# Attention scores: one 128-key product per head on half of the array's rows, in place of two 64-key products on quarters

## The chip, the cores and the metric

The kernel runs on one core of one Trainium2 chip. The metric is the device time of one execution in microseconds (us), lower is better. The engines of the core are named as in the profile: PE (TensorE, matrix products), PEld (its weight loads), DVE (VectorE), ACT (ScalarE), POOL (GpSimd) and SP (which issues most of the DMAs).

## The reference

A linear attention with a decay per head feeds a mixture of experts in two levels (4 groups of 4 experts, one expert per token). B=4, H=8, S=768, D=64; 3072 tokens of 512 features, hidden width 1024.

```python
for t in range(S):
    state = gamma * state + einsum('bhd,bhe->bhde', k[:, :, t], v[:, :, t])
    y[:, :, t] = scale * einsum('bhd,bhde->bhe', q[:, :, t], state)
x = y.transpose(0, 2, 1, 3).reshape(B * S, H * D)
# per token: best group g, best expert e in it, with softmax weights g_w and e_w
out[tok] = g_w * e_w * (relu(x[tok] @ w1[g, e]) @ w2[g, e])
```

## The kernel before

**Stages.** The attention stage fills about the first 105 us. After it the kernel goes through the 16 experts one by one: tokens are gathered, transposed and sent through the two products of the expert's network, each split into a high and a low half of 16 bits. The instruction order of every engine is written out by hand (`manual_schedule`), so each engine works through its queue in the order in which the Python code issues it.

**The attention stage.** The sequence is cut in chunks of 128 tokens. There are 12 steps `i` (NS2): each takes one chunk of two of the four batch rows, `u` = 0 and 1. A step's queries, keys and values arrive by DMA (`load`, issued three or four steps ahead). The heads are held as four pairs `p`; the two heads of a pair, `par` = 0 and 1, lie on partitions 0 to 63 and 64 to 127, because a head has 64 features. All products of this stage are of 32-bit floats, and the trace shows two matmul records (two passes) for each of them, with a weight load for each; transposes have one.

The parts of a step, in the names of the code and with their lines in the profile:

- `score_mm(i, u)` (L240) makes the products of keys and queries within a chunk, for one `u`. Keys are the stationary operand (weights), queries the moving one. The result lies with keys on partitions and queries along the columns, in one PSUM bank `sh[2u + par]` for each `par`.
- `score_mask` (L252, DVE) multiplies a bank by the causal mask `tri` into `pf`; two instructions of 128x512 for each call of `score_mm`. Where a key is later than the query, `tri` is 0.
- `value_out` (L304) multiplies `pf` with the values, `state_out` (L291) multiplies the queries with the carried state, both into `op`; `state_mm` (L266) adds the chunk to the state.
- `keys_mm` (L225) and `trans_mm` (L350) are transposes, `logits_mm` (L324) and `select_mm` (L337) make the router's logits. `tally` (L555) and `route` (L444, L446) place the tokens.

**The quarters.** In a chunk the first 64 keys matter to all 128 queries, the last 64 keys only to the last 64 queries. `score_mm` uses this: for each head it issues a product of 64 keys with 128 queries and one of 64 keys with 64 queries, and leaves out the quarter of late keys and early queries. Each product takes 64 rows (features) and 64 columns (keys) of the array, so the four products of a pair take its four quarters. The order of the keys on the partitions is turned by 64 for every second pair (`KEYS`, and `tri[:, 1]` for the mask), so that the longer products go to either column half in turn. A call issues 4 pairs x 2 x 2 = 16 products, 32 passes.

**The order around it.** In step `i` from 2 to 10 the queue of PE is: `score_mm(i+1, 0)`, now and then `tally` or late `select_mm`, `state_out(i, ·)` (not where a sequence begins), `score_mm(i+1, 1)`, `value_out(i, 0)`, `value_out(i, 1)`, `state_mm`, `logits_mm(i-1)`, transposes, `select_mm`. Steps 0 and 1 issue the two calls of the next step back to back. There are 24 calls of `score_mm` in all. The mask of a call is used by `value_out` one step later.

Of the kernel before, what the change touches and what calls it, by code (L numbers as in the profile page):

```python
# [22 lines left out]
P = 128  # L23
# [88 lines left out]
class Kernel:  # L112
# [115 lines left out]
    def score_mm(self, i, u):  # L228


        nc, s = self.nc, self.st[i]
        qT, kT = s["q"][:, u], s["k"][:, u]
        for p in range(4):
            for late in range(2):
                for par in range(2):
                    half = (late + p) % 2
                    rs = slice(64 * par, 64 * par + 64)
                    ks = p * P + 64 * half
                    cs = slice(p * P + 64 * late, p * P + P)
                    nc.tensor.matmul(  # L240
                        self.sh[2 * u + par][64 * half:64 * half + 64, cs], kT[rs, ks:ks + 64], qT[rs, cs],
                        start=True, stop=True, skip_group_check=True,
                    )

    def score_mask(self, i, u):
        nc, s = self.nc, self.st[i]
# [1315 lines left out]
```

## Time and profile before

| | |
|---|---|
| median of 3 runs | 398.45 us (397.72 to 401.91) |
| the profiled execution, its own time | 397.01 us |
| its span in the trace | 395.3 us |
| what lies around the span | 1.7 us |
| PE busy | 383.5 us, 97% of the span |
| DVE, ACT, POOL busy | 289.1, 224.0, 159.5 us |
| mean granted clock of PE | 0.997 |

The span is the time from the first to the last instruction in the trace. Matrix products overlap one another, and their ends are modelled; a group's busy time is the union of its records, and the distance from the first start of one group to the first start of the next is what the group took from PE. That distance is used below. The chain of work that ended last follows the execution back from its last instruction, at each step to what released it.

### The profile page before, as it was taken

The numbers are of one execution on the slowest core, as the hardware profiler recorded it, in microseconds if no ns is written. First come the engines' busy times: TensorE is split into PE (matmuls) and PEld (weight loads), VectorE is DVE, ScalarE is ACT, GpSimd is POOL, SyncE is SP. The second block draws the span as 40 slices with busy tenths as digits, with TensorE's granted clock in tenths as the row PEclk, the third lists the DMA queues.
The fourth block names the chain that finished last, engine by engine and source line by source line (L and its number), as shares of the span: only waits on it lengthen the run. The fifth ranks groups of instructions, "written<-read, shape, count | busy, mean of one in ns | idle before, by whom it ended". The sixth has DMA issues, their size and how long they took to land.

```text
span 395.3 us, 14260 instructions
## 1 busy us (share of the span) xinstructions
PE 383.5 (97%) x5945; PEld 324.0 (82%) x5977; DVE 289.1 (73%) x480; ACT 224.0 (57%) x342; POOL 159.5 (40%) x172
## 2 busy tenths in 40 slices
PE   8999999999999999999999999999999999999992
PEld 4889889878869878888888879797887978869791
DVE  3675776858879969795868686776978769788620
ACT  2234534534744766666666566676776767667620
POOL 5542669567866216141516234241530413412112
PEclk9999999999999999999999999999999999999998
DMA  7999999989656997777879797988879789796001
GB/s 258 373 341 327 331 359 299 309 296 292 211 208 230 338 354 270 243 266 257 271 263 269 254 318 265 295 299 307 289 265 347 275 309 312 271 330 247 30 24 49
DMA packets 38043, 107.24 MB, mean 271 GB/s; under 512 B 11416, under 2 KB 11544, under 8 KB 30549
## 3 DMA queue, kind: packets, MB, share of 16 engines
q1 hardware_dynamic: 28752, 92.52, 67.8%
q0 software_dynamic: 8928, 12.63, 9.2%
q8 instruction: 54, 0.88, 0.9%
q10 hardware_dynamic: 292, 1.08, 0.9%
q14 instruction: 17, 0.13, 0.1%
HBM read 94.18 MB, written 13.20 MB: 272 GB/s over the span
## 4 chain that ended last, share of the span: by engine, by line
PE 83%; issue 10%; POOL 3%; DMA 1%; DVE 1%; ACT 0%; POOLq 0%; SPq 0%; DVEq 0%; ACTq 0%
PE hps L918 20%; PE yps L1011 16%; PE hps L898 8%; PE yps L1016 6%; PE op L304 6%; PE sh L240 5%; PE yps L1004 3%; PE tpx L839 3%; PE op L291 3%; PE sh L350 3%; PE stp L266 2%; POOL out L1098 2%; PE log L337 1%; PE yps L955 1%; PE sh L324 1%
## 5 line engine op out<-in xcount | busy, mean ns | idle before, releaser
L786 DVE TENSOR_TENSOR wl<-wf,wh 128x1024 bf16<-128x1024 f32 x120 | 145.2, 1221 | 39.2 <-ACT wh L784 39.0
L784 ACT ACTIVATE wh<-wf 128x1024 f16<-128x1024 f32 (+1 forms) x136 | 133.6, 1002 | 1.5 <-DMA wf<-w2p 1.5
L918 PE MATMUL hps<-xbh,wh 128*128 128x0 bf16 x544 | 95.0, 241 | 0.0
L918 PE MATMUL hps<-xbh,wl 128*128 128x0 bf16 x544 | 95.0, 241 | 0.0
L1098 POOL DMA_INDIRECT out<-yo,mt x18 | 22.2, 1234 | 103.3 <-ACT yo L1078 100.6
L918 PEld LDWEIGHTS <-wh 128*128 128x128 f16 x640 | 58.6, 98 | 0.3 <-issue 0.2
L925 ACT ACTIVATE hh<-hps 128x256 bf16<-128x256 f32 (+16 forms) x68 | 34.2, 503 | 35.9 <-PE hps L918 35.7
L918 PEld LDWEIGHTS <-wl 128*128 128x128 bf16 x544 | 53.2, 98 | 0.3
L1016 PEld LDWEIGHTS <-wh 128*128 128x128 f16 x448 | 28.6, 97 | 24.9
L252 DVE TENSOR_TENSOR pf<-sh,tri 128x512 f32<-128x512 f32 x48 | 30.6, 685 | 23.5 <-PE op L304 8.7
L898 PE MATMUL hps<-xbl,wh 128*128 128x256 f16 (+13 forms) x448 | 47.7, 249 | 0.0
L1011 PE MATMUL yps<-wh,hl 128*128 128x512 f16 x112 | 42.5, 379 | 0.0
L1011 PE MATMUL yps<-wl,hh 128*128 128x512 bf16 x112 | 42.4, 379 | 0.0
L1011 PE MATMUL yps<-wh,hh 128*128 128x512 f16 x112 | 42.4, 378 | 0.0
L841 ACT ACTIVATE xbh<-tpx 128x512 bf16<-128x512 f32 (+14 forms) x32 | 16.7, 523 | 42.9 <-PE tpx L839 42.8
L821 POOL DMA_INDIRECT xg<-xd,mt x22 | 36.2, 1648 | 10.5 <-PE hps L898 3.0
L1016 PEld LDWEIGHTS <-wl 128*128 128x128 bf16 x448 | 28.6, 97 | 13.3
L928 DVE SCALAR_TENSOR_TENSOR hl<-hps,hh 128x216 f16<-128x216 f32 (+15 forms) x64 | 36.8, 575 | 2.8 <-ACT hh L925 2.7
L898 PEld LDWEIGHTS <-wh 128*128 128x128 f16 x448 | 38.2, 98 | 0.4
L1098 POOL DMA_INDIRECT out<-yo,gx x8 | 9.6, 1197 | 55.9 <-ACT yo L1078 41.2
L1016 PE MATMUL yps<-hh,wh 128*128 128x0 bf16 x448 | 31.8, 192 | 0.0
L1016 PE MATMUL yps<-hh,wl 128*128 128x0 bf16 x448 | 31.7, 192 | 0.0
(210 smaller groups left out, 640.9 us busy)
## 6 DMA issues: line engine op xcount, KB each, us to landing
wf<-w2p SPq DMA_DIRECT2D x29, 1024.0 KB, 7.1
wf<-w1p SPq DMA_DIRECT2D x28, 1024.0 KB, 6.9
lq<-qkv SPq DMA_DIRECT2D x24, 256.0 KB, 5.5
lk<-qkv SPq DMA_DIRECT2D x24, 256.0 KB, 5.5
lv<-qkv SPq DMA_DIRECT2D x24, 256.0 KB, 5.3
xd<-xr SPq DMA_DIRECT2D x22, 256.0 KB, 4.8
wf<-w1p SPq DMA_DIRECT2D x16, 256.0 KB, 5.7
wf<-w2p SPq DMA_DIRECT2D x8, 256.0 KB, 5.6
```

Of the source, the lines that this page charges most:

```text
L252: nc.vector.tensor_tensor(o, sc, tri, ALU.mult)
L304: nc.tensor.matmul(s["o"][par][64 * half:64 * half + 64, u, pp], s["vs"][:, u, hs], s["pf", u][:, par, p, :], start=(c == 0 and u == 0 and ...
L784: nc.scalar.activation(u["wh"][i][:, cs], u["wf"][i][:, cs], AF.Copy)
L786: (eng or nc.vector).tensor_tensor(u["wl"][i][:, cs], u["wf"][i][:, cs], u["wh"][i][:, cs], ALU.subtract)
L821: nc.gpsimd.indirect_dma_start(out=xg[0:r, i, :], out_offset=None, in_=self.xd[0:n, :], in_offset=bass.IndirectOffsetOnAxis(ap=mt[0:r, i, ...
L898: nc.tensor.matmul(hv[:, a, 0:w], l, xl[:, k, 0:w], start=(k == 0 and a == 0), stop=False, skip_group_check=True)
L918: nc.tensor.matmul(o, l[:, k, fs], m, start=(n == 0 and not arms), stop=(n == len(terms) - 1), skip_group_check=True,)
L925: nc.scalar.activation(hh[:, f, 0:W], hv[:, :, 0:W], AF.Relu)
L928: nc.vector.scalar_tensor_tensor(*rest)
L1011: nc.tensor.matmul(big, h[:, k, 0:P], w[k], start=(n == 0), stop=(n == 23))
L1016: nc.tensor.matmul(o, w[k][:, d * P:d * P + P], m, start=(n == 0 and d == 0), stop=(n == 23), skip_group_check=True,)
L1098: s = nc.gpsimd.indirect_dma_start(out=self.out, out_offset=bass.IndirectOffsetOnAxis(ap=mt[0:r, i, 0:1].bitcast(U32), axis=0), in_=yo[0:r ...
```

## The change

`score_mm` issues, for each pair and each `par`, one product of all 128 keys with all 128 queries. It takes 64 rows and all 128 columns of the array, so the two heads of a pair take its two row halves. A call issues 4 x 2 = 8 products instead of 16. The quarter of late keys and early queries is computed now, and the mask multiplies it by 0. The order of the keys (`KEYS`), the mask, the banks and all the rest are as before.

```diff
         for p in range(4):
-            for late in range(2):
-                for par in range(2):
-                    half = (late + p) % 2
-                    rs = slice(64 * par, 64 * par + 64)
-                    ks = p * P + 64 * half
-                    cs = slice(p * P + 64 * late, p * P + P)
-                    nc.tensor.matmul(
-                        self.sh[2 * u + par][64 * half:64 * half + 64, cs], kT[rs, ks:ks + 64], qT[rs, cs],
-                        start=True, stop=True, skip_group_check=True,
-                    )
+            for par in range(2):
+                rs, cs = slice(64 * par, 64 * par + 64), slice(p * P, p * P + P)
+                nc.tensor.matmul(
+                    self.sh[2 * u + par][:, cs], kT[rs, cs], qT[rs, cs], start=True, stop=True, skip_group_check=True
+                )
```

## Rows read from the trace of the kernel before

**Rows 1.** The page: busy time by engine, and the chain that ended last.
```profile
PE 383.5 (97%) x5945; PEld 324.0 (82%) x5977; DVE 289.1 (73%) x480; ACT 224.0 (57%) x342; POOL 159.5 (40%) x172
PE 83%; issue 10%; POOL 3%; DMA 1%; DVE 1%; ACT 0%; POOLq 0%; SPq 0%; DVEq 0%; ACTq 0%
```
**Rows 2.** Busy time (count) by window: PE, PEld, DVE, ACT, POOL; clock, DMA share, GB/s.
```profile
20.00:40.00 20.00, 20.00 (x460) 18.33 (x461) 13.15 (x26) 8.08 (x18) 6.55 (x7) 1.00 0.99 335
40.00:60.00 20.00, 19.42 (x456) 17.13 (x457) 14.84 (x45) 8.39 (x18) 13.61 (x21) 1.00 0.96 341
60.00:80.00 20.00, 20.00 (x466) 17.87 (x462) 15.17 (x39) 10.26 (x22) 15.33 (x23) 1.00 0.94 304
80.00:100.00 20.00, 19.02 (x409) 16.58 (x407) 14.31 (x45) 8.43 (x17) 14.48 (x20) 1.00 0.88 296
...
200.00:300.00 100.00, 100.00 (x1309) 83.90 (x1319) 75.94 (x85) 67.52 (x93) 35.32 (x24) 1.00 0.83 287
```
**Rows 3.** The chain of waits in time, 0 to 110 us: one step's part.
```profile
72.43 0.81 PE sh L240 x24
73.25 0.89 PE op L291 x32
74.14 0.65 PE sh L240 x24
74.79 1.91 PE op L304 x32
76.71 0.93 PE stp L266 x32
```
**Rows 4.** Groups by line and form, 0 to 180 us: busy us, mean ns.
```profile
L304 PE MATMUL op<-pf,vs 128*64 128x128 f32 x384 | 23.8, 276 | 0.0
L240 PE MATMUL sh<-lq,lk 64*64 64x128 f32 x384 | 21.5, 274 | 2.1 <-issue 1.3 <-DMA lk<-qkv 0.9
L304 PEld LDWEIGHTS op<-pf,vs 128*64 128x64 f32 x384 | 20.7, 137 | 1.9 <-POOL vs L197 0.8 <-issue 0.3
L240 PE MATMUL sh<-lq,lk 64*64 64x64 f32 x384 | 20.1, 222 | 0.0
L240 PEld LDWEIGHTS sh<-lq,lk 64*64 64x64 f32 x768 | 18.6, 133 | 4.3 <-issue 3.4 <-DMA lq<-qkv 0.4 <-DMA wf<-w2p 0.2
L337 PE MATMUL log<-rest,ls 128*128 128x20 f32 x48 | 6.8, 258 | 0.0
L337 PEld LDWEIGHTS log<-rest,ls 128*128 128x128 f32 x48 | 6.3, 191 | 0.7 <-ACT ls L329 0.2 <-issue 0.2
```
**Rows 5.** Timeline of PE in steps 7 and 8: start us, us, operation, count.
```profile
63.22 0.52 PE L337 MATMUL log<-rest,ls 128*128 128x20 f32 x4
63.67 0.90 PE L240 MATMUL sh<-lq,lk 64*64 64x128 f32 x32
64.50 0.45 PE L555 MATMUL log<-yT,hot 128*128 128x160 bf16 x4
64.88 1.10 PE L291 MATMUL op<-lq,V 64*64 64x128 f32 x32
65.80 0.85 PE L240 MATMUL sh<-lq,lk 64*64 64x128 f32 x32
66.58 1.97 PE L304 MATMUL op<-pf,vs 128*64 128x128 f32 x32
68.38 1.10 PE L266 MATMUL stp<-vs,kk 128*64 128x64 f32 x32
...
72.36 0.90 PE L240 MATMUL sh<-lq,lk 64*64 64x128 f32 x32
73.08 1.06 PE L291 MATMUL op<-lq,V 64*64 64x128 f32 x32
73.96 0.85 PE L240 MATMUL sh<-lq,lk 64*64 64x128 f32 x32
```
**Rows 6.** The same view: two calls back to back, and what follows.
```profile
12.03 1.57 PE L240 MATMUL sh<-lq,lk 64*64 64x128 f32 x64
13.53 0.66 PE L225 MATMUL log<-ident,lk 128*128 128x128 f32 x4
...
19.93 1.61 PE L240 MATMUL sh<-lq,lk 64*64 64x128 f32 x64
21.47 0.65 PE L225 MATMUL log<-ident,lk 128*128 128x128 f32 x4
...
56.52 1.57 PE L240 MATMUL sh<-lq,lk 64*64 64x128 f32 x64
58.02 1.97 PE L304 MATMUL op<-pf,vs 128*64 128x128 f32 x32
```
**Rows 7.** The same view: L304 and L291 groups of 16, before either kind of successor.
```profile
7.63 1.09 PE L304 MATMUL op<-pf,vs 128*64 128x128 f32 x16
8.66 0.90 PE L240 MATMUL sh<-lq,lk 64*64 64x128 f32 x32
...
10.59 1.05 PE L304 MATMUL op<-pf,vs 128*64 128x128 f32 x16
11.47 0.63 PE L266 MATMUL stp<-vs,kk 128*64 128x64 f32 x16
...
22.49 0.67 PE L291 MATMUL op<-lq,V 64*64 64x128 f32 x16
23.09 1.10 PE L350 MATMUL sh<-ident,xt 128*128 128x128 f32 x8
...
25.19 0.62 PE L291 MATMUL op<-lq,V 64*64 64x128 f32 x16
25.63 0.85 PE L240 MATMUL sh<-lq,lk 64*64 64x128 f32 x32
```
**Rows 8.** The same view: gaps inside a call, in brackets.
```profile
42.53 0.89 PE L240 MATMUL sh<-lq,lk 64*64 64x128 f32 x30 [0.34 <-issue]
...
83.18 0.71 PE L240 MATMUL sh<-lq,lk 64*64 64x128 f32 x22 [0.92 <-issue]
```
**Rows 9.** One line's instructions (L240): who waited for it, us and times.
```profile
  DVE pf L252: 7.6, 7
```

## The prediction

> **What bounds the kernel now.** I read the page first: PE is busy for 97% of the span and holds 83% of the chain that ended last, and no other engine passes 73% [rows 1]. That is an average over two very different stages, so the second view is the busy time by window. In the attention stage, where the change lies, PE is busy for 20.00, 19.42, 20.00 and 19.02 of each 20 us, DVE for at most 15.17, at a granted clock of 1.00, which is the 2.4 GHz level [rows 2]. Third, the chain in order of time: a step of attention is PE group after PE group with no other engine between them [rows 3]. So PE's own time sets the length of this stage, and what a call of `score_mm` adds or saves on PE goes into the end almost in full. The experts behind it are PE-bound too, 100.00 of 100 us busy [rows 2], so a shift of their start is not made good there.
>
> **What a call costs now.** I take it from PE's timeline, as the distance from the first start of its 32 passes to the first start of the next group. Followed by L291, which has the same form of array (64 rows times 64 columns), it is 72.36 to 73.08, 0.72 us; followed by L304 (128 times 64), 65.80 to 66.58, 0.78; followed by a group on the full array, 63.67 to 64.50, 0.83 [rows 5]. Of the 24 calls, five are of the first kind, eight of the second, five of the third. Six stand in pairs back to back: 12.03 to 13.53, 19.93 to 21.47, 56.52 to 58.02, 4.54 us for the three pairs [rows 6]. The sum: 5 x 0.72 + 8 x 0.78 + 5 x 0.83 + 4.54 = 18.5 us, 0.77 a call. This is all that the change can save.
>
> **What fills that time: the columns, or the number of instructions?** L291 is the test. It has 32 passes too, in the same four quarters, but all of 128 columns, and takes 73.08 to 73.96, 0.88 us [rows 5]. A quarter gets 8 of these passes, so one takes 0.88/8 = 110 ns while four quarters work at once. L304 gives the same for a column half: 16 passes in 66.58 to 68.38, 1.80 us, or 112 ns each [rows 5]. In a call of `score_mm` a quarter gets four passes of 128 columns and four of 64, so 4 x 110 + 4 x 55 = 0.66 us by this measure, against the 0.72 seen. The call is close to its column time; it is not held up by its instruction count.
>
> **The change, part by part.**
>
> *Fewer, longer products.* Removed are 32 passes a call, half of 128 and half of 64 columns [rows 4]; added are 16 of 128 columns, each on a row half. A row half gets 8 passes (4 pairs x 2). At L304's 112 ns that is 8 x 0.112 = 0.90 us if the two halves work at once. The busiest part of the array thus gets more columns than before: 8 x 128 = 1024, where a quarter had 4 x 128 + 4 x 64 = 768. Halving the instructions does not help; leaving the late-key quarter in costs a third more.
>
> *The weight loads.* A load now has 128 columns instead of 64. The nearest row is L337: its loads of 128 columns in 32-bit floats take 191 ns against 133 for L240's [rows 4], and its four passes of only 20 columns still need 63.22 to 63.67, 0.45 us or 112 ns each [rows 5]. There the load sets the pace, and it is the same 112 ns, so in the stream the load just fits behind the pass before it. From below this part costs nothing. From above, the first load of each call lies open for 191 - 133 = 58 ns longer, 24 x 0.058 = 1.4 us. I take nothing in the sum and keep 1.4 for the upper end.
>
> *Changes of the array's form.* No other group has the form of 64 rows times 128 columns. Before, a call shares its form with L291. The price of a change after passes of 128 columns: 16 passes of L304 take 10.59 to 11.47, 0.88 us, where L266 with the same form follows, and 7.63 to 8.66, 1.03 us, where L240 follows; 16 of L291 take 0.44 before L240 (25.19 to 25.63) and 0.60 before L350 (22.49 to 23.09) [rows 7]. So 0.15 to 0.16 us each. Now 21 of the 24 calls (all but the first of each back-to-back pair) are followed by another form: 21 x (0.90 + 0.15) + 3 x 0.90 = 24.7 us, against 18.5, or +6.2. And the eight L291 groups that were followed by a call in their own form now end in a change too: 8 x 0.16 = +1.3. The Trainium skill's page "TensorEngine Tiling (Array Packing)", section "Key Properties", says that a change of tiling mode, not just of tile, drains the engine, and this speaks against the change. By that rule every boundary counts, as in the sum of +7.5; were there no such price, it would be 24 x 0.90 - 18.5 = +3.1. The trace agrees with the rule: +0.15 us at the boundaries of rows 7.
>
> *Gaps inside calls.* Twice PE stops in the middle of a call for nothing that the profile shows, 0.34 and 0.92 us [rows 8]. If that is the arrival of instructions, fewer of them may shorten it: between 0 and -1.3 us. I take -0.5.
>
> *What is hidden.* The mask's work is unchanged, and its output is needed a step later. DVE waits 7.6 us in seven waits for the scores as it is [rows 9]; it will start some 0.2 to 0.3 us later and has at least 4.8 of each 20 us free [rows 2]. Without that slack the delay would reach `value_out` a step later. DMAs, banks, waits and the order of the queues stay.
>
> **The sum.** +6.2 + 1.3 - 0.5 = +7.0 with every change of form at its price, +3.1 - 0.5 = +2.6 if these changes cost nothing. I am nearer to the first, since the boundary price was seen on two lines, but a part of it may be a wait for the next group's own data and not a drain: +6. On the profiled execution's 397.0 us that is 403.0. The median of the three runs shown is 398.45, some 1.4 above that execution, which would give 404.4. I predict 403.5, a slowdown of 1.3%.
>
> **The rivals.**
>
> *1. The two row halves do not overlap.* No group of this trace uses row halves with all columns, so this is not shown. Each call then takes 16 x 0.112 = 1.79 us, 21 x (1.79 + 0.15) + 3 x 1.79 = 46.1, or +27.6, with L291's 1.3 about +29: 426 us. For it: each half now writes all 128 partitions of its bank. Against it: L291 gets through 32 passes in 0.88 us [rows 5], so row halves must already work at once there, writing the same partitions of two banks. Chance 0.09.
>
> *2. Form changes are mostly hidden, and the gaps shrink.* Then the calls cost only their columns: between 24 x 8 x 0.110 - 18.5 - 1.3 = +1.3 and +3.1 with nothing off: 398.3 to 400.1 on the profiled execution, about 399.5 to 401.5 against the median, within 1% all the same. For it: a call's own change to L304 costs only 0.78 - 0.72 = 0.06 us today [rows 5]. Against it: those calls end in short passes. Chance 0.25.
>
> *3. The instructions set the pace, and the kernel gets faster.* If today's 0.77 us were the price of 32 passes and 32 loads, half of them would need 0.39: 24 x 0.39 + 21 x 0.15 + 1.3 - 18.5 = -4.7 us, 392.3. It decides from the point where a 128-column pass takes less than (18.5 - 3.2 - 1.3)/(24 x 8) = 73 ns. Against it: L291 has the same count as a call and takes 0.88 where the call takes 0.72 [rows 5], so columns count and instructions do not. Chance 0.05. The Trainium skill's page "TensorE: Matmul & The Clock Gate", section "Wait — 56ns, not 53.3ns?", gives a floor of about 25 ns between starts however few the columns; by it 32 passes need 0.80 us and 16 need 0.40, an estimate that would favour this rival. The trace does not agree: 0.72/32 is 22.5 ns.
>
> **How the numbers follow.** The forecast, +3.5 to +9 us, has the rest, 0.61. About 1% is what a measurement of this kernel can tell from no change, here 394.5 to 402.4 us. Slower by more than that takes rival 1, and of the forecast all but its lowest part: 0.09 + 0.57 = 0.66. Faster takes most of rival 3: 0.04. The rest, 0.30, is within 1%. The range reaches from rival 2, 399.0, to the sum with all boundary prices and the open first loads (7.5 + 1.4 = +8.9 on 398.45, 407.4) and a little over for a load that does not quite fit: 410.0. It leaves out rivals 1 and 3 and the lowest of rival 2.
>
> **What would show it.** In the profile after, L240 should have 384 passes and as many loads, of the form 64 rows times 128 columns; a call should take 0.90 us before its neighbour in form and 1.00 to 1.10 before another; L291 before L240 should go from 0.88 to about 1.04; the experts' first products should start some 6 us later; and DVE and POOL should stay as busy as they are. A call of 1.8 us would be rival 1; 0.9 with no rise at the boundaries rival 2; under 0.6 rival 3. The prediction is wrong at the root if calls get longer and the start of the experts does not move: then PE was not what bounds this stage.

## The result and the profile after

The changed kernel takes 404.46 us (median of 6 runs, 403.81 to 409.92) against 399.35 us of the kernel before (6 runs, 397.72 to 401.91). The ratio is 1.0126, with a 95% interval of 1.0101 to 1.0152. One run of the changed kernel, the one of 409.92, was disturbed and is not in the ratio. The prediction was 403.5, in a range of 399.0 to 410.0, with the most weight on slower by more than 1%.

The profiled execution took 404.13 us, its span is 402.4 us. First the page's busy times; they answer to [rows 1].

```profile
PE 388.8 (97%) x5518; PEld 329.1 (82%) x5593; DVE 289.0 (72%) x480; ACT 224.0 (56%) x342; POOL 159.5 (40%) x172
```

PEld has 384 records fewer, and PE is busy 5.3 us longer. DVE, ACT and POOL do what they did. The line of `score_mm` (L236 now; every line behind it moved up by 5) has half the passes and half the loads, all of one form:

```profile
L236 PEld LDWEIGHTS sh<-lq,lk x384: 182/188/188, 4.8 to 95.7; 64*128 64x128 f32 x192
L236 PE MATMUL sh<-lq,lk x384: 272/272/373, 4.8 to 95.8; 64*128 64x128 f32 x192
```

The three numbers are the shortest, median and longest duration in ns. A load took 133 ns in the mean [rows 4], and the median is 188 now. Most passes take 272, the first of a call 373.

Next PE's timeline in steps 3, 6 and 7 (start us, us, operation, count), against [rows 5] and [rows 6]:

```profile
33.22 1.16 PE L236 MATMUL sh<-lq,lk 64*128 64x128 f32 x16
34.31 1.10 PE L286 MATMUL op<-lq,V 64*64 64x128 f32 x32
35.35 1.16 PE L236 MATMUL sh<-lq,lk 64*128 64x128 f32 x16
36.44 1.97 PE L299 MATMUL op<-pf,vs 128*64 128x128 f32 x32
...
59.28 2.06 PE L236 MATMUL sh<-lq,lk 64*128 64x128 f32 x32
61.27 1.97 PE L299 MATMUL op<-pf,vs 128*64 128x128 f32 x32
...
66.92 1.16 PE L236 MATMUL sh<-lq,lk 64*128 64x128 f32 x16
68.01 0.45 PE L550 MATMUL log<-yT,hot 128*128 128x160 bf16 x4
```

A call is 33.22 to 34.31, 1.09 us, and it is 1.09 whatever form follows. Two calls back to back take 59.28 to 61.27, 1.99, so the first of them takes 0.90. The product with the state (L286) in front of a call takes 34.31 to 35.35, 1.04, where it took 0.88 [rows 5]. Over all 24 calls the distances add up to 25.6 us. Before they were 18.5 without the gaps (18.7 with the last call, whose first passes mix with the group ahead of it).

The windows show that PE still bounds the stage (PE, PEld, DVE, ACT, POOL busy; clock, DMA share, GB/s), against [rows 2]:

```profile
20.00:40.00 20.00, 20.00 (x345) 17.69 (x344) 10.86 (x20) 6.08 (x13) 6.93 (x7) 1.00 0.94 311
60.00:80.00 20.00, 20.00 (x353) 17.91 (x353) 14.34 (x43) 8.86 (x19) 14.07 (x21) 1.00 0.90 307
```

The first expert's products start at 110.02 us instead of 105.13 (the kernel before, then the changed one):

```profile
105.13 0.22 PE L918 MATMUL hps<-xbh,wh 128*128 128x0 bf16 x1
110.02 0.22 PE L913 MATMUL hps<-xbh,wh 128*128 128x0 bf16 x1
```

That is 4.9 us later, but the calls and L286 alone add 8.1 (7.1 and 1.0). And the span grew by 7.1 us, more than the start of the experts moved. Both remainders had to be explained.

### The profile page after: what moved, and what is told of

It is laid out like the page before. It is cut to its first block, busy times and chain, and to the rows that moved or that the text cites. A ratio compares the mean times of both kernels' runs of the same rounds, so it can differ in the third digit from the quotient of the medians.

```text
span 402.4 us, 13449 instructions
## 1 busy us (share of the span) xinstructions
PE 388.8 (97%) x5518; PEld 329.1 (82%) x5593; DVE 289.0 (72%) x480; ACT 224.0 (56%) x342; POOL 159.5 (40%) x172
## 4 chain that ended last, share of the span: by engine, by line
PE 79%; issue 13%; POOL 3%; DVE 1%; DMA 1%; ACT 1%; POOLq 0%; SPq 0%; DVEq 0%; ACTq 0%
PE hps L913 19%; PE yps L1006 12%; PE hps L893 8%; PE yps L1011 7%; PE sh L236 6%; PE op L299 5%; PE yps L999 3%; PE tpx L834 3%; PE op L286 3%; PE sh L345 2%; PE stp L261 2%; POOL out L1093 2%; PE log L332 1%; PE yps L950 1%; PE sh L319 1%
## 5 line engine op out<-in xcount | busy, mean ns | idle before, releaser
L913 PE MATMUL hps<-xbh,wh 128*128 128x0 bf16 x544 | 95.2, 241 | 0.9 <-issue 0.9
L913 PE MATMUL hps<-xbh,wl 128*128 128x0 bf16 x544 | 95.3, 241 | 0.4 <-issue 0.4
L913 PEld LDWEIGHTS <-wh 128*128 128x128 f16 x640 | 58.5, 98 | 0.4
L913 PEld LDWEIGHTS <-wl 128*128 128x128 bf16 x544 | 53.1, 98 | 2.1 <-issue 1.9
L247 DVE TENSOR_TENSOR pf<-sh,tri 128x512 f32<-128x512 f32 x48 | 30.6, 685 | 28.5 <-PE sh L236 10.9
L197 POOL TENSOR_TENSOR vs<-lv,cst 128x512 f32<-128x512 f32 x24 | 24.6, 1043 | 15.6 <-DMA lv<-qkv 9.8
```

The source lines that it names most:

```text
L197: self.nc.gpsimd.tensor_tensor(o, v, g, ALU.mult)
L247: nc.vector.tensor_tensor(o, sc, tri, ALU.mult)
L913: nc.tensor.matmul(o, l[:, k, fs], m, start=(n == 0 and not arms), stop=(n == len(terms) - 1), skip_group_check=True,)
```

## The experiments

The theory to be tested: a call takes what the busiest part of the array has to stream, plus an entry and an exit where the form of the array changes. Rivals: only the new form costs, not the columns; the row halves work in turn; the number of instructions sets the pace. Beside that stood the question of the gaps that end with no releaser.

**Columns without the new form.** Both products of a head take all 128 queries, still on quarters.

```diff
-                    cs = slice(p * P + 64 * late, p * P + P)
+                    cs = slice(p * P, p * P + P)
```

> The kernel before, with only the columns changed: both products of a head take all 128 queries, on quarters of the array as before, 32 passes a call. The count of instructions and the changes of form stay as they were. Theory 1 (the busiest part of the array sets a call: 8 passes of 128 columns, plus the entry and exit of a form): a call takes 0.88 us before L291, about 1.03 before another form, the 24 calls together about 23.5 us against 18.5 before, so the attention stage is some 5 us longer than before and L291 keeps its 0.88; the total 402 to 405 us, near the changed kernel. Theory 2 (what the change costs is the new form of array alone, with its loads of 128 columns and its boundaries): calls stay at 0.72 to 0.83 and the total within 1 us of before, about 399.

401.28 us (10 runs) against 398.40 (13 runs), ratio 1.006, interval 1.0027 to 1.0092. PE's timeline of this kernel, steps 2 and 3:

```profile
25.74 0.62 PE L291 MATMUL op<-lq,V 64*64 64x128 f32 x16
26.18 1.05 PE L240 MATMUL sh<-lq,lk 64*64 64x128 f32 x32
27.16 1.97 PE L304 MATMUL op<-pf,vs 128*64 128x128 f32 x32
...
32.81 1.10 PE L240 MATMUL sh<-lq,lk 64*64 64x128 f32 x32
33.73 1.05 PE L291 MATMUL op<-lq,V 64*64 64x128 f32 x32
```

A call takes 0.92 before L291 and 0.98 before L304. The 24 calls sum to 23.4 us without one stop; 23.5 was expected. L291 keeps its 0.44 for 16 passes in front of a call. So the columns alone account for +4.9 of the +7.1 us of the changed kernel's calls, and the form for the other 2.2 and the 1.0 on L286. The theory holds and the rival that only the form costs falls. The total, 401.28, lies below the 402 to 405 that were expected; by the ratio it is 2.4 us longer. The last part of this section says why.

**The order of the row halves.** The changed kernel with its two loops turned: all pairs of one half, then all of the other.

```diff
-        for p in range(4):
-            for par in range(2):
+        for par in range(2):
+            for p in range(4):
```

> The changed kernel with the order of its 8 products turned: all four pairs of one row half first, then all four of the other. The work is the same. Theory 1 (the row halves work at once, and only because neighbouring instructions go to different halves): now they can't overlap, a call takes 16 x 0.112 = 1.79 us plus about 0.2 for entry and exit, some 0.9 more for each of 24 calls, +21 us, about 425. Theory 2 (passes are taken out of order, or the halves never overlapped): a call stays at 1.09 and the total at 404.

423.17 us in one run against 398.40. PE's timeline in step 2:

```profile
34.57 1.71 PE L236 MATMUL sh<-lq,lk 64*128 64x128 f32 x16
36.21 0.67 PE L286 MATMUL op<-lq,V 64*64 64x128 f32 x16
```

The call takes 34.57 to 36.21, 1.64 us, neither the 1.99 of no overlap at all nor 1.09. The same 16 passes with the halves in turn take 0.55 us less, so in the changed kernel the two row halves do work at once, and it is the order of the instructions that lets them. The run is 24.8 us above the kernel before. Of these the changed kernel's own loss is about 5, and 18 x 0.55 + 3 x 0.76 = 12.2 are the longer calls (a pair takes 2.75 instead of 1.99). Another 7 us were lost ahead of step 2, where all of PE's work was slow; the last section comes back to that. So it is partly luck that the total lies so near the 425 of theory 1.

**The boundary, taken away.** The changed kernel with both calls of a step behind the two `state_out`.

```diff
-                if i > 1:
-                    scores(i + 1, 0)
...
                 if i > 1:
+                    scores(i + 1, 0)
                     scores(i + 1, 1)
```

> The changed kernel with the two calls of a step back to back, after both L291 groups and not around them. One change of form fewer in each of eight steps; the products are the same. Theory 1 (a call pays about 0.19 us for entering and leaving its form): the first call of each pair takes 0.90 us and the second 1.09, eight times 0.19 = 1.5 us less than the changed kernel, about 403. Theory 2 (the 0.19 is a wait for banks or for the mask, not for the form): the second call starts no earlier, the total stays at 404.5, or grows because the masks of both calls now come together on DVE.

405.22 us against 398.40, ratio 1.0155, interval 1.0092 to 1.0217. On PE, step 2, a pair takes 1.98 us, and the 24 calls 24.0 instead of 25.6, which is what was expected. But the total did not fall. The waits of PE say where it went (us in total, times, longest):

```profile
PE log L550 <- POOL yT L529: 1.9, 3, 0.8
PE op L286 <- ACT xr L353: 0.4, 1, 0.4
```

Neither wait is in the changed kernel. With the first call gone from the start of the step, `tally` (L550) comes at PE before POOL has made its entries.

**The same with the tally behind the calls.** One move more, to take that wait away.

```diff
-                if i in (5, 7, 9):
-                    self.tally()
...
                     scores(i + 1, 1)
+                if i in (5, 7, 9):
+                    self.tally()
```

> The changed kernel with the two calls of a step back to back, as in the run before, and the tally of the token lists (three times) moved behind them. With the calls paired alone, the 24 calls took 1.6 us less (24.0 against 25.6), but PE waited 0.83, 0.27 and 0.83 us for POOL's entries ahead of the tally, and the total did not fall. Theory 1 (the form's price is real and was only handed on to that wait): the waits go, the total is 1 to 2 us under the changed kernel's, 402.5 to 403.5. Theory 2 (something else gives the 1.6 us back): the total stays at 404.5 to 405.

402.15 us against 396.29 on that chip, ratio 1.0144, interval 1.0109 to 1.018: not clearly different from the changed kernel's 1.0126. The waits for POOL are gone; these stand in the list now:

```profile
PE sh L345 <- ACT ls L324: 0.5, 1, 0.5
PE op L286 <- DVE xt L311: 0.4, 1, 0.4
PE log L439 <- DVE oh L403: 0.3, 1, 0.3
```

In the changed kernel the first of them is 0.2 and the other two are 0.1 or nothing. From the L299 of step 2 to the first expert's product it needs 82.1 us, the changed kernel 82.5: of some 1.4 us saved there about 0.3 are left and 0.9 went into these waits. The theory of the boundary price is right on PE. That the price can be had back by pairing the calls is not; the first call stood where it covered other engines.

**Half the columns.** The changed kernel with the last 64 queries of a chunk alone; the first 64 get no scores, so only the attention stage can be read.

```diff
+                qs = slice(p * P + 64, p * P + P)
                 nc.tensor.matmul(
-                    self.sh[2 * u + par][:, cs], kT[rs, cs], qT[rs, cs], start=True, stop=True, skip_group_check=True
+                    self.sh[2 * u + par][:, qs], kT[rs, cs], qT[rs, qs], start=True, stop=True, skip_group_check=True
                 )
```

> The changed kernel with the scores of the last 64 queries of each chunk alone: products of 128 keys and 64 queries on row halves; the scores of the first 64 queries are left out, so the routing differs and only the attention stage can be read. Theory 1 (in a stream of passes of 128 columns a load of 128 columns of weights just fits, so loads set the pace as soon as the passes get shorter): a pass stays at about 112 ns, a call at 0.95 to 1.05 us. Theory 2 (the columns set the pace alone): 8 x 0.056 = 0.45 plus 0.2 for entry and exit, 0.65 us a call.

One run, 432.93 us, with another routing in the experts. PE's timeline in step 2:

```profile
30.16 1.11 PE L237 MATMUL sh<-lq,lk 64*128 64x64 f32 x16
31.20 0.67 PE L287 MATMUL op<-lq,V 64*64 64x128 f32 x16
```

A call takes 1.04 us with half the columns, against 1.09. In both kernels the loads of a row half start 112 ns apart all through a call, and the median pass takes 272 ns in both. So in this form the columns streamed do not set the pace alone; loads of 128 columns, which the call has in common with L337 and its 112 ns [rows 5], are the reading that fits, though no run changed the width of the loads by itself. Here columns that could be left out would gain next to nothing. So two limits stand at the same height for the 0.90 us of the changed kernel's eight passes: the first experiment shows that the columns alone reach it on quarters, and this one that on row halves nearly all of it stays when half of the columns go.

**More and shorter products.** The opposite step from the kernel before: four products of 32 keys per head on strips of 32 columns, with only the queries that they can matter to.

```diff
-            for late in range(2):
+            for late in range(4):
...
-                    half = (late + p) % 2
-                    ks = p * P + 64 * half
-                    cs = slice(p * P + 64 * late, p * P + P)
+                    j = (late + p) % 4
+                    ks = p * P + 32 * j
+                    cs = slice(p * P + 32 * late, p * P + P)
```

> The opposite step from the kernel before: four products of 32 keys per head, with the 128, 96, 64 and 32 queries that those keys can matter to, on eighths of the array (64 rows, 32 columns). The order of the keys is turned by 32 from pair to pair, so each column strip gets 320 columns in two passes each; the mask follows in 16 bits. A call has 64 passes and 64 loads instead of 32 and 32. Theory 1 (the columns of the busiest part set a call): 2 x 320 columns at 110 ns for 128 are 0.55 us, plus 0.1 as in the kernel before, 0.65 us a call, 24 x 0.12 = 3 us less, 395 to 397. Theory 2 (the number of instructions sets a call): twice the 0.72 to 0.83 of the kernel before, about 1.5 us a call, +17 us, about 416. Between: at the 11 ns for an instruction that the kernel before shows (64 in 0.72 us), 128 need 1.4 us.

423.78 us against 395.87, ratio 1.0722, interval 1.0673 to 1.0771. PE's timeline in steps 2 and 3:

```profile
32.99 1.04 PE L240 MATMUL sh<-lq,lk 64*32 64x128 f32 x64
33.95 0.67 PE L290 MATMUL op<-lq,V 64*64 64x128 f32 x16
...
43.17 0.84 PE L240 MATMUL sh<-lq,lk 64*32 64x128 f32 x36
46.47 0.57 PE L240 MATMUL sh<-lq,lk 64*32 64x96 f32 x28 [2.47 <-issue]
```

An undisturbed call takes 0.97 us, more than the 0.65 by its columns and less than the 1.4 by its instructions, so both forecasts fall. The total is lost elsewhere. PE stops inside its groups, for nothing that the profile shows:

```profile
PE sh L240 <- issue: 4.5, 4, 2.5
PE op L290 <- issue: 4.0, 3, 1.8
PE stp L265 <- issue: 3.5, 5, 1.6
```

That is 12.0 us in twelve stops, in the trace of an execution of 418.85 us. Two smaller losses come with it. PE waits 2.1 us for POOL ahead of the first L303, because this mask takes 16 instructions of POOL to set up and not 3. And the granted clock falls twice to 0.50, the 1.2 GHz level, from 10.67 to 14.08 and from 20.91 to 24.32 us, after PE had stood idle for 2.09 us up to 9.54 and for 1.80 up to 20.12.

**The stops: by code or by execution?** The kernel before had three such stops in attention, two of them in score calls [rows 8]; the changed kernel none there, but some in the experts. First the changed kernel with 96 small products more at the start of PE's queue, which puts 192 instructions ahead of all its other work.

```diff
-        for i in range(WARM):
-            nc.tensor.matmul(warm, one[:, 0:P], one, start=True, stop=True)
+        for i in range(105):
+            nc.tensor.matmul(warm[:, 0:32], one[:, 0:P], one[:, 0:32], start=True, stop=True)
```

> The changed kernel, with the 9 warming products of 512 columns at the start replaced by 105 of 32 columns, so that 192 more instructions stand ahead of everything on PE; the work behind them is the same. The changed kernel has four gaps on PE between 125 and 136 us that end with no releaser, 1.5 us by the gaps and 2.6 by the shift of what follows; the kernel before had three others at 14.9, 42.5 and 83.2 us and none there. Theory 1 (they are the arrival of instructions, and depend on where the code lies in what is fetched): the gaps move or go, and the total changes by 1 to 3 us either way while calls keep their 1.09. Theory 2 (they come from work that is late at this point): gaps of the same size at the same lines, total unchanged within 0.5 us.

407.41 us against 398.40, ratio 1.0226, interval 1.0151 to 1.0302. The total does not answer the question, but the places do in part: the stops behind the first experts are 1.8 us by the shift of what follows them, instead of 2.6, and stand at the same products (L913) as before. So they do not go with a place in PE's queue. The rest of the loss is at the start, where a call takes twice as long (start us, us, operation):

```profile
4.59 2.08 PE L236 MATMUL sh<-lq,lk 64*128 64x128 f32 x16 [0.80 <-DMA lk<-qkv]
```

The small products were no equal of the warming ones. So both kernels were traced again, unchanged, twice.

> The kernel before once more, unchanged, for a second trace of it. In its first trace PE stops three times inside attention groups (at 14.9, 42.5 and 83.2 us; the groups take 0.79, 0.76 and 1.29 us more than their like) and not in the experts; the four other kernels that were traced stop three or four times about 5.8 us after the first transposes of the second group of experts' tokens, +2.0 and +0.6 us. Theory 1 (where PE runs short of instructions differs from execution to execution): the second trace has other stops, perhaps those in the experts, and a span 1 to 3 us from 395.3. Theory 2 (the stops belong to the kernel's code): the same three at the same groups, span within 0.5 us of 395.3.

> The changed kernel once more, unchanged, for a second trace of it. All that belongs to the products should repeat: 1.09 us a call before another form, 0.90 before a second call, 25.6 us for the 24 calls, 1.03 us for L286 before a call. Theory 1 of the stops (execution by execution): some other than those at 125.4 to 135.8 us. Theory 2 (by code): the same, +2.6 us in the experts. Span 402 to 403 us either way.

> The kernel before a third time, for its stops. Two traces gave stops inside attention groups that cost 2.8 and about 3.7 us over their like, at different places, and none in the experts. Theory 1 (64 instructions a call bring PE near the end of what is delivered, so attention stops in most executions): 2 to 4 us of stops in attention again, at other places, span 395 to 397. Theory 2 (the stops are rare chance): under 1 us, span 393 or less.

> The changed kernel a third time, for its stops. Its two traces gave 0 and 0.6 us of stops inside attention, 2.6 and 0 in the experts. Theory 1 (half the instructions in the score calls leave attention nearly without stops): under 1 us in attention again; the experts may or may not stop. Theory 2 (chance): 2 to 4 us in attention as in the kernel before. Calls 1.09 and 25.6 us in all either way.

They took 397.78 and 397.80 us (before), 402.43 and 404.12 us (changed). From each trace, in us: attention from the first score to the first expert's product; the experts from there to the end of the span; and the stops inside attention, as the excess of a group over others of its kind.

| | attention | of it stops | experts | span |
|---|---|---|---|---|
| before, 1st trace | 99.97 | 2.8 | 290.1 | 395.3 |
| before, 2nd | 100.62 | 3.7 | 289.9 | 396.0 |
| before, 3rd | 99.26 | 1.6 | 292.0 | 396.0 |
| changed, 1st trace | 105.20 | 0 | 292.4 | 402.4 |
| changed, 2nd | 105.93 | 0.7 | 289.7 | 400.7 |
| changed, 3rd | 105.22 | 0.2 | 292.5 | 402.4 |

The 24 calls without stops and L286 repeat within 0.1 us in each kernel's traces, but for the first call, which took 1.55 instead of 1.09 in the second trace of the changed kernel and 1.35 instead of 0.83 in the third of the kernel before. One stop of the kernel before comes in all three traces, after four passes of the first L291 group; the others move. In its second trace the one cost 1.9 and another 1.3 us (timeline, a gap in brackets).

```profile
14.52 0.44 PE L291 MATMUL op<-lq,V 64*64 64x128 f32 x4
16.42 1.09 PE L291 MATMUL op<-lq,V 64*64 64x128 f32 x28 [1.46 <-issue]
...
27.10 0.27 PE L240 MATMUL sh<-lq,lk 64*64 64x128 f32 x1
28.36 0.90 PE L240 MATMUL sh<-lq,lk 64*64 64x128 f32 x31 [0.99 <-issue]
```

The stops of the experts are there or not, in either kernel, and cost some 2.5 us where they are. The waits of the third trace of the kernel before, which its first had not:

```profile
PE hps L918 <- issue: 1.3, 3, 0.5
PE tpy L1093 <- issue: 0.3, 1, 0.3
```

The second traces of both kernels were taken on one chip and have none; the third traces were taken on another and both have them. Four other kernels traced on a third chip have them too. So the experts' stops are no effect of the change. The first pair of traces had compared an execution without them with one that had them. What they are stays open.

The stops in attention are another matter. In the three traces of the kernel before there are 1.6 to 3.7 us of them, in the changed kernel 0 to 0.7, and those 0.7 and 0.2 stand at the L299 of the last step, 8 us behind the last score call. Over the kernels they rise with the density of the score calls: 32 loads and passes in 1.09 us, 0.3 us of stops (mean of three traces); 64 in 0.92 (all queries on quarters), 0.6 in a score call (one trace); 64 in 0.77, 2.7 (mean of three); 128 in 0.97, some 15 by this measure (one trace). This is also why the first experiment cost only 2.6 us in attention: 4.9 us more for the calls, about 2 us less of stops.

The traces say more about the cause than this order. The kernel before has 7 of these stops with a gap of over 0.1 us in its three traces, all queries on quarters has one, and the eighths have 12. Counted in the instructions of PE's queue, all 20 lie at places that are 256, or a multiple of 256, apart (to within two). All 20 end 2.2 to 3.3 us after a transfer of 16 KB begins on the instruction queue q8, and 1.2 to 1.6 us after it is over. There is one such transfer for about 250 instructions of PE. In the first 105 us the kernel before has 17 and the changed kernel 13 (transfers, MB, share of the 16 DMA engines' time):

```profile
q8 instruction: 17, 0.28, 1.1%
q8 instruction: 13, 0.21, 0.8%
```

So, as far as traces can show it, PE stops there because its next instructions come too late. None of the eight traces with 32 loads and passes to a call has a stop of this kind in attention. Why some transfers begin in time and others do not stays open, and no experiment changed the delivery by itself.

No version tried is faster than the kernel before.

## Why the prediction was right, point by point

- **PE bounds the stage.** Right: PE is busy 20.00, 19.76, 20.00 and 19.89 of each 20 us from 20 to 100 us, and the later start of the experts goes into the end. In the mean of three traces each attention is 5.5 us longer (105.45 against 99.95).
- **Columns, not the count of products.** Right, and shown by the first experiment: +4.9 us from the columns alone. A pass in the stream was put at 112 ns; two calls back to back give 0.90 for 8 passes, exactly that. On row halves this is not the columns' doing alone, since half the columns left a call at 1.04 us.
- **The row halves work at once.** Right: 1.09 us a call, and 1.64 where the order of the instructions hinders them. Rival 1 falls.
- **The load of 128 columns.** In the stream it fits behind the pass, as taken, and seems to have nothing to spare: half the columns left the pace where it was. At the start of a call it lies open: the first pass takes 373 ns against 272, and against 320 in the changed kernel's L286 groups after a change of form. The 1.09 us of a call is 0.04 over the 1.05 of the sum, the greater part of the 0.058 us that stood only at the upper end of the range. This term was mis-sized: nothing was taken, about 21 x 0.04 = 0.9 us came.
- **Changes of form.** 25.6 us for the calls against 24.7 in the sum, the difference being the load above. The L291 groups in front of a call cost +1.0 in all, not +1.3: some of them took 0.92 before and not 0.88, as their own entry was open already. Every call pays at its boundary, the same 0.19 us (1.09 - 0.90) whatever form follows; in the paired calls the first takes 0.90. Rival 2 falls. The Trainium skill's page "TensorEngine Tiling (Array Packing)", section "Key Properties", has a drain at each change of mode, and the trace agrees.
- **The gaps inside calls.** This step failed in size. It took -0.5 and held -1.3 for the end of it, from the two gaps of [rows 8]. A group with a gap loses more than the gap itself: 14.12 to 15.94, 41.81 to 43.35 and 81.75 to 83.82 cost 2.8 us together, and the first of them, in L291, was not counted at all. The three traces give 2.7 us before and 0.3 after, so -2.4. The reason that was offered with an "if", the arrival of instructions, is the one that the traces bear out.
- **What is hidden.** Right: DVE waits longer for the scores than before [rows 9], 10.9 us in ten waits, and PE waits nowhere for DVE. Who waited for L236:

```profile
  DVE pf L247: 10.9, 10
```

- **The sum.** 7.1 + 1.0 - 2.4 = +5.7, against +5.5 in attention. Predicted were 6.2 + 1.3 - 0.5 = 7.0, brought down to 6 with the argument that a part of the boundary price may be a wait for data. That argument was wrong: the price was paid in full. The reduction came out near the truth by luck, because the stops, which were put too low, gave the time back. By +6 the forecast would have been 404.4, and 404.46 was measured; the last 0.9 us, down to 403.5, were taken off without a reason.
- **Rival 3, the instructions.** It fell as a rule for the length of a call: 64 loads and passes take 0.72 or 0.92 us, and 128 take 0.97. The floor of about 25 ns between starts, which the Trainium skill's page "TensorE: Matmul & The Clock Gate", section "Wait — 56ns, not 53.3ns?", gives, is not seen here: 64 passes in 0.97 us are 15 ns each. But its core was not empty: the stops come where PE's next instructions arrive too late, and with half the instructions in the calls they shrank by 2.4 us, against the 8.1 us that the calls and L286 cost. In the kernel with eighths they are the greater part of the loss.

## What to carry to other kernels

Count the columns that the busiest part of the array has to stream, and those that it has to load, not the products: joining two small products into one on twice the array gains nothing if the part that was fullest gets fuller, and any form of array that the neighbours don't share is paid for at every boundary. Smaller and denser instructions have a limit of their own: look for gaps inside groups that end with no releaser, and measure what such a group loses against its like, not the gap alone. Before two traces are compared stage by stage, take a second one of each, both on the same chip: here 2.5 us came and went in the experts without any change.

## What was not expected of the hardware

- The stops described above, each at a transfer of PE's instructions: some 15 us in the kernel with 128 loads and passes to a call, 2.7 in the mean with 64 in the kernel before, and none of this kind with 32.
- In four traces (the turned row halves, half the columns, the small warming products, the pairs with the late tally) the first calls took nearly twice their time, 2.01 us instead of 1.09 in the pairs with the late tally. The window view gives a granted clock of 1.00 for these stretches, but it counts 1.00 wherever the trace has no clock record, and in these traces the record begins only at 20.20, 16.80, 13.40 and 16.14 us. The groups go to their usual length at these moments. In the other traces it begins between 3.4 and 6.0 us, and the two long first calls noted above lie across its beginning (6.02 and 5.90 us). What the clock was before is not recorded, but four transposes of L225 take 1.11 us in these stretches, as in the kernel with eighths at a recorded clock of 0.50, and 0.66 elsewhere. So these were stretches at the lower level, 1.2 GHz, as far as the lengths tell. The rows: the pairs with the late tally, the eighths, and the eighths' window with its clock.

```profile
7.39 1.11 PE L225 MATMUL log<-ident,lk 128*128 128x128 f32 x4
12.08 1.11 PE L225 MATMUL log<-ident,lk 128*128 128x128 f32 x4
10.67:14.08 3.41, 3.41 (x86) 2.79 (x87) 1.29 (x2) 0.60 (x1) 1.90 (x2) 0.50 1.05 381
```

  Why the clock rose so late in these executions, with the same nine warming products as elsewhere in three of them, stays open. The profiled execution of the pairs with the late tally took 406.23 us, its four other runs 401.62 to 402.37.
